# Delta-rule attention and a mixture of depths on one core: Gram matrices spilled from small buffers, corner blocks read back, inverses turned on VectorE, the first batches' experts last

## Chip, cores and metric

The kernel runs on one core of a Trainium2 chip. The metric is the device time of one execution in microseconds (us), the median of several runs.

## What is computed

The first block is a delta-rule recurrence over 768 steps for each of 4 batches and 8 heads, with a 48 x 48 state per head. The second gives the 128 best-scored tokens of each batch to a two-layer expert.

```python
k_n = k / (np.linalg.norm(k, axis=-1, keepdims=True) + 1e-06)
for t in range(S):                                   # state: (B, H, D, D)
    y[:, :, t] = einsum('bhd,bhde->bhe', q[:, :, t], state)
    v_old = einsum('bhde,bhd->bhe', state, kt)
    state = state + bt * einsum('bhd,bhe->bhde', kt, vt - v_old)
x = y.transpose(0, 2, 1, 3).reshape(B, S, H * D)     # (4, 768, 384)
scores = einsum('bsd,d->bs', x, w_gate)
for b in range(B):
    top = np.argpartition(-scores[b], 128)[:128]
    ye = np.maximum(x[b, top] @ w1, 0.0) @ w2        # 384 -> 1024 -> 384
    out[b, top] = x[b, top] + sigmoid(scores[b, top])[:, None] * ye
```

## The kernel before

**Units.** The sequence is cut into 12 chunks of 64 steps, and the batches into two groups (0 and 1, then 2 and 3). A unit `i` (0 to 23) is one chunk of one group: 16 pairs of batch and head, two to the 128 partitions. Within a chunk the delta rule is a triangular system. Its 64 x 64 matrix is inverted in two halves of 32: two 32 x 32 diagonal blocks and a corner block that couples them.

**Stages of a unit.** `prep` (L442) loads k and q, transposes them on TensorE (L433), forms the Gram matrix of k (`products`, L487; unit 0 to 3: `mm_g0`, L464 to L471), copies it to `g` (`out_g`, L494) and spills it to DRAM (`spill`, L499); it also forms q times k and masks it on VectorE (`out_p`, L503, into `p`). `eliminate` (L539) inverts the diagonal blocks of four units at once, so there are six eliminations, 0 to 5. It reads the blocks from DRAM with row and block index exchanged (`turn_in`, L553, into `a`; elimination 0 transposes on VectorE, L548), scales them (L559 to L584; a square root on ScalarE, L563), has ScalarE copy them into the PSUM bank pair `ap` (`lift`, L588) and runs 30 steps of a multiply and a subtract on VectorE (L600, L607). `final` (L613) multiplies by a table `mb` that GpSimd writes (L577), and `turn_out` (L616) transposes into `tt`. The inverse is needed in the other orientation too (`turn_back`): eliminations 0 and 5 transpose once more on VectorE (L621); eliminations 1 to 4 send it to DRAM (`ad`, L625) and back into `g` (`bring`, L630), and a third transfer copies the low blocks inside `tt` (`move`, L635). These three are called the round trip below. `join` (L670) makes the corner of the inverse for each unit with two products on TensorE, z (L692, L694) and j (L705, L707), and ScalarE copies (`ej`, L714). `recur` (L731) is the recurrence: R (L753, state times k), the add on VectorE (L760), W (L766, the inverse times v), ScalarE copies (L771), S (L777, the new state), copies (L784), and Q and P for the output (L793, L804, L810). Unit i needs unit i - 1's state.

**Ranking and experts.** Each unit's scores are taken (L827 on GpSimd, L831 on ScalarE) and compared with all earlier ones (`ranking`: rank products L898 and L900, compares L912 and L916 on GpSimd, L919 and L923 on VectorE, sums L940). Behind a group's last chunk its 128 tokens per batch are chosen (L982) and turned into indices by a product (L1000). `depths(b)` runs the expert of one batch: gather (L1021), turn (L1027), first product (L1037), second product (L1051), result (L1056), scatter (L1061).

**What sets the order.** All of this is entered as operations in a planner (`Plan`). Each has an engine, a duration, a priority and the ring buffers that it takes and gives back; the planner simulates the engines and writes each engine's instructions in one fixed order. Where TensorE would be idle it puts matmuls on a constant tile `warm` (fillers, L343). At run time each engine's queue is in order, and semaphores hold an instruction until its inputs are there.

**Buffers that matter here.** `g` has two places, each the Grams of a whole elimination, and a place is given back by the last join of that elimination (L670 on). `a` and `gd` have two places as well, `ad` two, `mb` one, `inv` three PSUM banks. `xe` (gathered tokens) has two places.

Of the kernel before, what the change touches and what calls it, by code (L numbers as in the profile page):

```python
# [15 lines left out]
P = 128  # L16
# [169 lines left out]
def kernel(  # L186
# [57 lines left out]
    ring("g", 2, [NB, C])  # L244
    ring("a", 2, [HC, HC])
    rings["gd"] = [dram.tile([P, NB, C], FP32, name=f"gd{m}") for m in range(2)]
    rings["ad"] = [dram.tile([2, HC, NB, HC], FP32, name=f"ad{m}") for m in range(2)]
    plan.ring("gd", 2)
    plan.ring("ad", 2)
    ring("mb", 1, [HC, HC])  # L250
# [8 lines left out]
    ring("xe", 2, [DM])  # L259
# [11 lines left out]
    plan.ring("boot", 2)  # L271

# [19 lines left out]
    bnat = const.tile([B * H, S], FP32, name="bnat")  # L292
# [60 lines left out]
    def constants():  # L353
# [13 lines left out]
        for t in rings["tt"]:  # L367
            nc.gpsimd.memset(t[:, :, :HC], 0.0)
# [73 lines left out]
    def prep(i):  # L442
# [32 lines left out]
        def out_g0(rt):  # L475
            def emit():
                nc.scalar.copy(
                    got("g", e)[:, n0:n0 + GP].rearrange("p (r b) t -> p r b t", b=2)[:, :, rt],
                    got(*kb)[rt][:, :GI * C].rearrange("p (r t) -> p r t", t=C))
            return emit  # L480
# [11 lines left out]
        def out_g(rt):  # L492
            def emit():
                nc.scalar.copy(got("g", e)[:, n0:n0 + GP]  # L494
                               .rearrange("p (r b) t -> p r b t", b=2)[:, :, rt], bank(kg[rt]))
# [27 lines left out]
        if first:  # L523
            n["g"] = pe(1.5, mm_g0, [n["ek"]], u, take=[kb] + [("g", e)] * (i == 0), hard=True,
                        ins=40 * GI)
            n["eg"] = [act(0.38, out_g0(rt), [n["g"]], u, give=[kb], hard=True)
                       for rt in range(2)]
        else:
            n["g"] = pe(0.55, products("kt", kg), [n["ek"], N[e * BC].get("g")], u, ins=16 * GI,
                        take=kg + [("g", e)] * (i % BC == 0))  # L530
            n["eg"] = [act(0.38, out_g(rt), [n["g"]], u, give=[kg[rt]]) for rt in range(2)]
            n["sg"] = sp(0.45, spill, n["eg"], u, take=[("gd", e)] * (i % BC == 0), moves=0.7,
                         dmas=1)
        v = 10 * i - 14
# [4 lines left out]
    def eliminate(e):  # L539
# [3 lines left out]
        near = first or e == NE - 1  # L543
        hard = dict(hard=first)

        def turn_in():
            if first:
                nc.vector.transpose(out=got("a", e),  # L548
                                    in_=got("g", e)[:, :, HC:].rearrange("p n t -> p t n"))
                return  # L550
            for par in range(2):
                for hf, rows in ((0, lo[par]), (1, hi[par])):
# [3 lines left out]
                        .rearrange("p n t -> n p t"))  # L556

# [70 lines left out]
        def bring():  # L628
            for par in range(2):
                nc.sync.dma_start(out=got("g", e)[lo[par], :, :HC], in_=got("ad", e)[par])  # L630

        def move():
            t = got("tt", e)
            for par in range(2):
                nc.sync.dma_start(out=t[lo[par], :, :HC], in_=t[lo[par], :, HC:])  # L635
# [4 lines left out]
        else:  # L640
            ti = sp(2.6, turn_in, [N[i]["sg"] for i in range(e * BC, (e + 1) * BC)], u,
                    take=[("a", e)], give=[("gd", e)], dmas=4, moves=0.83)
# [15 lines left out]
        last = dve(1.15, final, [last, s["mb"]], u, give=[] if near else [("mb", e)], **hard)  # L658
        N["final", e] = last
        s["to"] = dve(1.95, turn_out, [last], u, take=[("tt", e)], give=[("a", e)], **hard)  # L660
        if near:
            s["tb"] = dve(2.05, turn_back, [last], u, give=[("a", e)], hard=True)
        else:
            tb = sp(1.25, turn_back, [last], u, take=[("ad", e)], give=[("a", e)], dmas=2, moves=0.83)
            s["tb"] = sp(1.25, bring, [tb], u, give=[("ad", e)], dmas=2, moves=0.83)
# [475 lines left out]
```

## Time and profile before

| | us |
|---|---|
| median of 3 runs | 340.2 (338.43 to 340.38) |
| the profiled execution's own time | 336.96 |
| its span, first to last instruction | 335.2 |
| TensorE busy in the span | 308.9 |
| VectorE busy in the span | 207.6 |
| ScalarE busy in the span | 185.2 |
| GpSimd busy in the span | 104.4 |

In the profile PE is TensorE's matmuls, PEld its weight loads, DVE VectorE, ACT ScalarE, POOL GpSimd, and SP the SyncE queue that issues most DMAs. A row of groups names line, engine and operation, output and input tiles, shapes and count; then busy us and the mean of one in ns; then the engine's idle time just before, with what ended it. Busy matmuls overlap in their pipeline, so their busy time is more than their share of the queue.

### The profile page before, as it was taken

To read this page: it belongs to the slowest core of one execution; us is meant where nothing else is said; L and a number is where in the kernel's file an instruction comes from. 1 tells how busy PE (TensorE), PEld (TensorE's weight loads), DVE (VectorE), ACT (ScalarE), POOL (GpSimd) and SP (SyncE) were. 2 spreads that over 40 slices of the span, in tenths; PEclk is the share of its full clock that TensorE was granted. 3 is DMA by queue.
4 is the path that set the end of the run, shared out by engine and by line. 5 is a ranking of instruction groups with operands and counts; after the bars stand their busy time and mean duration, and the time that the engine had idled before them with its cause. 6 is when DMAs were issued, how large, how long until landed. Compare 5 with 4: busy or idle time off the path is not lost.

```text
span 335.2 us, 15324 instructions
## 1 busy us (share of the span) xinstructions
PE 308.9 (92%) x6678; PEld 231.5 (69%) x6678; DVE 207.6 (62%) x576; ACT 185.2 (55%) x508; POOL 104.4 (31%) x150
## 2 busy tenths in 40 slices
PE   7779999999879999989987999789999999999994
PEld 3665445788656778678864889656976888656782
DVE  6047998879769981798879796798840311252000
ACT  2445006776654666876785867863396688500110
POOL 8204001321360224404794232422021254802011
PEclk9969999999959999999977999989999999999998
DMA  7977991357793479767887268940050111201000
GB/s 132 140 130 184 179 344 42 56 137 176 126 170 62 94 178 164 134 132 195 158 151 135 55 176 151 164 89 10 23 117 7 43 34 49 49 2 47 2 23 23
DMA packets 130483, 35.89 MB, mean 107 GB/s; under 512 B 122832, under 2 KB 127056, under 8 KB 130416
## 3 DMA queue, kind: packets, MB, share of 16 engines
q1 hardware_dynamic: 127792, 32.95, 47.7%
q0 software_dynamic: 512, 1.57, 1.5%
q8 instruction: 52, 0.85, 1.0%
q10 hardware_dynamic: 2112, 0.39, 0.7%
q14 instruction: 15, 0.12, 0.1%
HBM read 22.05 MB, written 11.80 MB: 101 GB/s over the span
## 4 chain that ended last, share of the span: by engine, by line
PE 69%; ACT 10%; issue 7%; DVE 6%; POOL 4%; DMA 2%; SPq 0%; POOLq 0%; ACTq 0%; DVEq 0%
PE inv L343 16%; PE inv L433 7%; PE inv L487 7%; PE prec L766 6%; PE inv L1051 5%; PE psta L777 5%; PE prec L753 4%; PE inv L1037 4%; PE py L804 4%; PE py L793 3%; POOL mk L912 3%; ACT wbd L771 2%; DVE ap L607 2%; DVE tmp L600 2%; ACT tt L714 2%
## 5 line engine op out<-in xcount | busy, mean ns | idle before, releaser
L343 PE MATMUL inv<-warm 128*128 128x512 bf16 x282 | 71.8, 395 | 2.2 <-DVE warm L357 2.1
L607 DVE TENSOR_TENSOR ap<-ap,tmp 128x30 f32<-128x30 f32 (+9 forms) x180 | 60.7, 337 | 5.4
L600 DVE TENSOR_TENSOR tmp<-a,ap 128x30 f32<-128x30 f32 (+9 forms) x180 | 58.7, 326 | 5.4
L745 POOL TENSOR_TENSOR v<-v,nnT 128x384 f32<-128x384 f32 x24 | 20.0, 840 | 97.7 <-DMA v<-in_v_dram 61.5
L343 PEld LDWEIGHTS <-warm 128*128 128x128 bf16 x282 | 26.6, 101 | 30.0 <-issue 3.2
L827 POOL TENSOR_TENSOR prod<-x,wg 128x384 f32<-128x384 f32 x22 | 23.0, 1044 | 32.9 <-ACT x L810 28.4
L912 POOL TENSOR_SCALAR mk<-rep 128x64 bf16<-128x64 f32 (+11 forms) x22 | 27.5, 1249 | 15.9 <-ACT rep L904 8.2
L771 ACT COPY wbd<-prec 64x384 f32<-64x384 f32 x48 | 22.6, 472 | 14.1 <-PE prec L766 12.5
L714 ACT COPY tt<-inv 32x128 f32<-32x128 f32 x96 | 24.5, 255 | 9.0 <-PE inv L707 7.4
L760 DVE TENSOR_TENSOR v<-v,prec 128x384 f32<-128x384 f32 x22 | 12.2, 552 | 26.8 <-ACT x L810 15.0
L766 PE MATMUL prec<-v,tt 64*64 64x48 f32 x768 | 27.4, 220 | 0.7 <-DVE v L760 0.7
L766 PEld LDWEIGHTS prec<-v,tt 64*64 64x64 f32 x768 | 24.4, 134 | 5.2 <-DVE v L760 3.6
L1051 PE MATMUL inv<-w_sb,hT 128*128 128x384 f32 x64 | 24.2, 521 | 0.3 <-ACT tt L714 0.3
L784 ACT COPY s<-psta 64x384 f32<-64x384 f32 x44 | 20.8, 472 | 3.8 <-PE psta L777 3.2
L777 PE MATMUL psta<-wbd,k 128*48 128x96 f32 x352 | 19.1, 251 | 3.9 <-ACT wbd L771 3.5
L1037 PE MATMUL inv<-xeT,w_sb 128*128 128x128 f32 x192 | 22.5, 277 | 0.0
L1037 PEld LDWEIGHTS inv<-xeT,w_sb 128*128 128x128 f32 x192 | 21.7, 192 | 1.0 <-ACT xeT L1031 0.9
L503 DVE TENSOR_TENSOR p<-inv,up 128x256 f32<-128x256 f32 x48 | 19.1, 416 | 4.6 <-PE inv L487 3.2
L1056 DVE SCALAR_TENSOR_TENSOR oe<-inv,gate,xe 128x384 f32<-128x384 f32 x4 | 2.5, 618 | 31.0 <-PE inv L1051 31.0
L438 ACT COPY kt<-inv 128x512 f32<-128x512 f32 x24 | 14.0, 588 | 12.1 <-PE inv L433 12.0
L777 PEld LDWEIGHTS psta<-wbd,k 128*48 128x48 f32 x352 | 14.6, 122 | 8.7 <-ACT wbd L771 7.9
L804 PE MATMUL py<-wbd,p 128*64 128x96 f32 x384 | 20.5, 249 | 0.0
(142 smaller groups left out, 584.0 us busy)
## 6 DMA issues: line engine op xcount, KB each, us to landing
gd<-g SPq DMA_DIRECT2D x20, 256.0 KB, 3.1
v<-in_v_dram SPq DMA_DIRECT2D x48, 96.0 KB, 3.5
q<-in_q_dram SPq DMA_DIRECT2D x48, 96.0 KB, 3.4
k<-in_k_dram SPq DMA_DIRECT2D x44, 96.0 KB, 3.8
out_dram<-x SPq DMA_DIRECT2D x20, 192.0 KB, 2.8
a<-gd SPq DMA_DIRECT2D x20, 128.0 KB, 3.5
w_sb<-in_moe_w_dram SPq DMA_DIRECT2D x3, 512.0 KB, 4.5
w_sb<-in_moe_w_dram SPq DMA_DIRECT2D x4, 384.0 KB, 7.6
```

Source lines behind the costliest of these rows:

```text
L343: nc.tensor.matmul(rings[name][k], lhsT=warm[:, :P], rhs=warm, start=True, stop=True)
L433: nc.tensor.transpose(ps[:, r * P:(r + 1) * P], x[:, 2 * r:2 * r + 2].rearrange("p b d -> p (b d)"), ident)
L600: nc.vector.tensor_tensor(out=view(), op=ALU.mult, in0=got("a", e)[:, j + 1:, j:j + 1].to_broadcast([P, w, j]), in1=blocks[:, j:j + 1, :j] ...
L607: nc.vector.tensor_tensor(out=a[:, j + 1:, :j], in0=a[:, j + 1:, :j], in1=view(), op=ALU.subtract)
L714: nc.scalar.copy(to[lo[par], :, int(w == "jb"), HC:], view(w)[lo[par]])
L766: nc.tensor.matmul(pw[half[par], a], lhsT=tt[half[par], ch * GP + a], rhs=x[half[par], a], start=True, stop=True)
L771: nc.scalar.copy(wb[half[par], :, par], pw[half[par]])
L777: nc.tensor.matmul(psta[ds[a % 2], a // 2], lhsT=t[:, a, :D], rhs=wb[:, a].rearrange("p h d -> p (h d)"), start=(c == 0 and a < 2), stop=True,
L804: nc.tensor.matmul(pyv[half[bb], h4, rt], lhsT=t[:, a], rhs=wb[:, a], start=(c == 0 and h4 == 0 and rt == 0), stop=True, skip_group_check= ...
L912: nc.gpsimd.tensor_scalar(out=mk[:, :(j + 1) * C].rearrange("p (j c) -> p j c", c=C), in0=rep[:, :j + 1, :C], scalar1=rep[:, j, C:], scala ...
L1037: nc.tensor.matmul(got("inv", b, "h", f // 4)[:, f % 4 * CAP:(f % 4 + 1) * CAP], lhsT=w1_sb[:, t, f * P:(f + 1) * P], rhs=got("xeT", b)[:, ...
L1051: nc.tensor.matmul(got("inv", b, "o")[:CAP, :DM], lhsT=got("hT", b)[:, f], rhs=w2_sb[:, f], start=(f == 0), stop=(f == KF - 1))
```

## The change

Four things are changed.

1. The Grams of a unit go to one of four small places (`gs`, one unit each) and are spilled from there; a small place is free when its spill has landed. `gd` has a place for each elimination. Elimination 0's Grams lie in the second buffer of `tt`, whose low half GpSimd clears once their corners are used (`zeros`).
2. The corner blocks are read back from `gd` into `off` (`corner`), four DMAs an elimination, behind the `a` read.
3. The round trip is gone: in all eliminations VectorE transposes the inverse back into `mb` (two places now), and GpSimd copies the low blocks inside `tt` (`lows`, two copies a join; ScalarE did this in eliminations 0 and 5).
4. The experts of batches 0 and 1 get the priorities 400 to 406, behind everything, take the bank pair `ap` (ring `late`) and wait for the last elimination's `final`. `xe` has four places, so their tokens can be gathered early.

```diff
+    ring("gs", 4, [GP, C])
+    ring("off", 2, [BC * GI, HC])
     ring("a", 2, [HC, HC])
-    rings["gd"] = [dram.tile([P, NB, C], FP32, name=f"gd{m}") for m in range(2)]
...
+    rings["gd"] = [dram.tile([P, NB, C], FP32, name=f"gd{m}") for m in range(NE)]
...
+    rings["late"] = [ap[:, m] for m in range(2)]
+    plan.ring("late", 2)
+    first_g = rings["tt"][1]
...
         def spill():
-            nc.sync.dma_start(out=got("gd", e)[:, n0:n0 + GP], in_=got("g", e)[:, n0:n0 + GP])
+            nc.sync.dma_start(out=got("gd", e)[:, n0:n0 + GP], in_=got("gs", i))
...
+        def corner():
+            for par in range(2):
+                for rows, at, cols in ((hi[par], 0, slice(0, HC)), (lo[par], 1, slice(HC, C))):
+                    nc.sync.dma_start(out=got("off", e)[rows], in_=got("gd", e)[rows, at::2, cols])
...
         def turn_back():
-            if near:
-                nc.vector.transpose(out=got("mb", e).rearrange("p n t -> p t n"),
-                                    in_=got("a", e).rearrange("p i c -> p c i"))
-                return
-            for par in range(2):
-                nc.sync.dma_start(out=got("ad", e)[par].rearrange("i n k -> n i k"),
-                                  in_=got("a", e)[lo[par]])
...
+            nc.vector.transpose(out=got("mb", e).rearrange("p n t -> p t n"),
+                                in_=got("a", e).rearrange("p i c -> p c i"))
...
         def lows():
             t = got("tt", e)[:, n0:n0 + GP]
             for par in range(2):
-                nc.scalar.copy(t[lo[par], :, :HC], t[lo[par], :, HC:])
...
+                nc.gpsimd.tensor_copy(t[lo[par], :, :HC], t[lo[par], :, HC:])
...
-        u += du
...
+        u = u + du if g == NG - 1 else 400 + 4 * bb
+        tx = pe(0.4, turn_x, [ga] + [N["final", NE - 1]] * (g < NG - 1), u, take=[(bk, b, "xt"), ("xeT", b)], give=[("xe", b)],
```

SyncE, as elimination 2 ends, before: `a_107` is elimination 2's block, `a_108` elimination 3's, `gd_109` their spilled Grams.

```order
L499 DMA gd_109<-g_106 128x512
L422 DMA q_77<-in_q_dram 64x8x48 x2
L625 DMA ad_112<-a_107 32x32x32 x2
L815 DMA out_dram<-x_118 64x2x384 x2
L635 DMA tt_116<-tt_116 32x32x32 x2
L553 DMA a_108<-gd_109 32x32x32 x4
L630 DMA g_105<-ad_112 32x32x32 x2
L422 DMA k_69<-in_k_dram 64x8x48 x2
```

The same place after: `a_112` is elimination 3's block, `gd_115` its Grams, `off` the corners.

```order
L503 DMA gd_115<-gs_108 128x512
L426 DMA k_68<-in_k_dram 64x8x48 x2
L426 DMA q_76<-in_q_dram 64x8x48 x2
L812 DMA out_dram<-x_125 64x2x384 x2
L426 DMA q_77<-in_q_dram 64x8x48 x2
L556 DMA a_112<-gd_115 32x32x32 x4
L426 DMA k_69<-in_k_dram 64x8x48 x2
L426 DMA v_78<-in_v_dram 64x8x48 x2
L426 DMA q_75<-in_q_dram 64x8x48 x2
L564 DMA off_109<-gd_115 32x16x32 x4
```

The read of elimination 3's block stood behind two transfers that wait for elimination 2's end; now none of these is left, and the corners follow a few loads later.

VectorE, from the last steps of elimination 3 on, before (`a_108` is elimination 3's block, `a_107` elimination 4's, L760 the recurrence's add):

```order
L600 TENSOR_TENSOR tmp<-a_108,ap 128x30
L607 TENSOR_TENSOR ap<-ap,tmp 128x30
L613 TENSOR_TENSOR a_108<-ap,mb_113 128x1024
L616 STREAM_TRANSPOSE tt_117<-a_108 128x32x32
L946 TENSOR_TENSOR csum_154<-csum_154,inv_130 128x8
L559 TENSOR_SCALAR nrm<-a_107 128x32
```

The same place after (`a_112` is elimination 3's block, `a_111` elimination 4's; L575 to L579 are the small scalings, L592 is the scaling of the block):

```order
L579 TENSOR_TENSOR bh_168<-bh_168,bt 128x32
L615 TENSOR_TENSOR ap<-ap,tmp 128x30
L757 TENSOR_TENSOR v_83<-v_83,prec 128x384
L621 TENSOR_TENSOR a_112<-ap,mb_120 128x1024
L582 STREAM_TRANSPOSE nnT_166<-nrm 128x32
L624 STREAM_TRANSPOSE tt_124<-a_112 128x32x32
L628 STREAM_TRANSPOSE mb_120<-a_112 128x32x32
L592 TENSOR_TENSOR a_111<-a_111,bh_168 128x1024
```

Elimination 4's diagonal and small scalings have moved ahead of elimination 3's last step; the second transposition has come in.

TensorE behind the last W, after (W is L763; `ap` is written by the experts of batches 0 and 1, L1035 and L1049; before, fillers stood in these gaps):

```order
L763 MATMUL prec<-v_83,tt_124 64x48 x16
L895 MATMUL inv_138<-spr_128,pair 128x2x64
L897 MATMUL inv_138<-scr_158,ident 128x2
L790 MATMUL py<-s_173,qt_100 64x2x48 x8
L1049 MATMUL ap<-w_sb,hT_134 128x384
L801 MATMUL py<-wbd_172,p_104 64x96 x8
L895 MATMUL inv_137<-spr_128,pair 128x64
L897 MATMUL inv_137<-scr_158,ident 128x1
L1049 MATMUL ap<-w_sb,hT_134 128x384 x2
L1025 MATMUL ap<-ident,both 128x128 x3
```

Parts of the two late experts now stand between the rank products; the planner places 207 fillers in all, where it placed 282.

## Rows read from the trace of the kernel before

**Rows 1.** The page's first part: busy us (share of span) x instructions.

```profile
PE 308.9 (92%) x6678; PEld 231.5 (69%) x6678; DVE 207.6 (62%) x576; ACT 185.2 (55%) x508; POOL 104.4 (31%) x150
```

**Rows 2.** Windows: elimination 0's last transposition to elimination 5's.

```profile
core 0: us, PE busy (x) PEld busy (x) DVE busy (x) ACT busy (x) POOL busy (x), PEclk, DMA share, GB/s
54.30:245.60 191.30, 176.63 (x4574) 141.82 (x4572) 154.75 (x428) 130.33 (x358) 64.58 (x68) 0.96 0.60 122
```

**Rows 3.** Groups of TensorE in the window 54.3 to 245.6.

```profile
L343 PE MATMUL inv<-warm 128*128 128x512 bf16 x64 | 20.1, 420 | 0.1
...
L1037 PE MATMUL inv<-xeT,w_sb 128*128 128x128 f32 x96 | 11.2, 277 | 0.0
...
L1051 PE MATMUL inv<-w_sb,hT 128*128 128x384 f32 x16 | 7.1, 593 | 0.3 <-ACT tt L714 0.3
```

**Rows 4.** Groups of VectorE in the window 54.3 to 245.6.

```profile
L607 DVE TENSOR_TENSOR ap<-ap,tmp 128x30 f32<-128x30 f32 (+9 forms) x150 | 50.5, 337 | 4.4
L600 DVE TENSOR_TENSOR tmp<-a,ap 128x30 f32<-128x30 f32 (+9 forms) x150 | 48.9, 326 | 4.4
L503 DVE TENSOR_TENSOR p<-inv,up 128x256 f32<-128x256 f32 x39 | 15.7, 414 | 1.8 <-ACT mute L930 1.3 <-PE inv L487 0.4
...
L760 DVE TENSOR_TENSOR v<-v,prec 128x384 f32<-128x384 f32 x16 | 8.8, 552 | 8.4 <-ACT rep L904 3.9 <-PE prec L753 3.7 <-DMA v<-in_v_dram 0.5
...
L559 DVE TENSOR_SCALAR nrm<-a 128x32 f32<-128x32 f32 x4 | 0.7, 184 | 7.0 <-DMA a<-gd 7.0
L591 DVE MEMSET ap<- 128x32 f32 x5 | 0.4, 85 | 5.0 <-ACT ap L588 5.0
```

**Rows 5.** Timeline of VectorE: start, us, what, idle before.

```profile
52.29 2.00 DVE L621 STREAM_TRANSPOSE mb<-a 128x1024 f32<-128x1024 f32 x1
...
122.52 1.94 DVE L616 STREAM_TRANSPOSE tt<-a 128x1024 f32<-128x1024 f32 x1
...
133.90 0.19 DVE L559 TENSOR_SCALAR nrm<-a 128x32 f32<-128x32 f32 x1 [3.64 <-DMA a<-gd]
...
243.48 2.09 DVE L621 STREAM_TRANSPOSE mb<-a 128x1024 f32<-128x1024 f32 x1
```

**Rows 6.** DMA issues of the round trip: KB each, us to landing.

```profile
ad<-a SPq DMA_DIRECT2D x8, 128.0 KB, 3.4
...
g<-ad SPq DMA_DIRECT2D x8, 128.0 KB, 3.5
```

**Rows 7.** Timeline of TensorE: W of units 0, 20 and 23.

```profile
57.49 1.27 PE L766 MATMUL prec<-v,tt 64*64 64x48 f32 x32
...
267.13 1.08 PE L766 MATMUL prec<-v,tt 64*64 64x48 f32 x30
...
285.22 1.13 PE L766 MATMUL prec<-v,tt 64*64 64x48 f32 x32
```

**Rows 8.** TensorE from 285.2 on: the fillers' group, then timeline rows.

```profile
L343 PE MATMUL inv<-warm 128*128 128x512 bf16 x68 | 16.2, 379 | 0.0
...
306.67 0.49 PE L1027 MATMUL inv<-ident,xe 128*128 128x128 f32 x3
...
307.73 5.62 PE L1037 MATMUL inv<-xeT,w_sb 128*128 128x128 f32 x48
...
324.93 5.33 PE L1051 MATMUL inv<-w_sb,hT 128*128 128x384 f32 x16
```

**Rows 9.** Timeline: VectorE's scaling alone and beside GpSimd's table.

```profile
55.86 1.22 DVE L584 TENSOR_TENSOR a<-a,bh 128x1024 f32<-128x1024 f32 x1
...
92.42 1.26 POOL L577 TENSOR_SCALAR_AFFINE_SELECT mb<-bh 128x1024 f32<-128x1024 f32 x1 [3.67 <-DMA q<-in_q_dram]
...
92.73 2.02 DVE L584 TENSOR_TENSOR a<-a,bh 128x1024 f32<-128x1024 f32 x1
```

**Rows 10.** Groups of GpSimd by form: a fill of 1024 and a compare of 256.

```profile
L368 POOL MEMSET tt<- 128x1024 f32 x2 | 1.8, 950 | 0.0
...
L912 POOL TENSOR_SCALAR mk<-rep 128x256 bf16<-128x256 f32 x2 | 1.8, 920 | 0.0
```

More of the change, by code (lines that the diff above doesn't have):

```diff
@@ L258 @@
     ring("sel", 1, [NCH, CAP], BF16)
-    ring("xe", 2, [DM])
+    both = sbuf("both", [B, DM])
+    rings["xe"] = [both[:, m] for m in range(B)]
+    plan.ring("xe", B)
+    bnat = both[:B * H, :2].rearrange("p m d -> p (m d)")
+    assert S == 2 * DM
     ring("xeT", 1, [KD, CAP])
@@ L533, in prep @@
                          dmas=1)
+            plan.add("DMA", 0.0, lambda: None, [n["sg"]], u, give=[("gs", i)])
         v = 10 * i - 14
@@ L657, in eliminate, with zeros @@
         N["steps", e] = last
-        last = dve(1.15, final, [last, s["mb"]], u, give=[] if near else [("mb", e)], **hard)
+        last = dve(1.15, final, [last, s["mb"]], u, **hard)
         N["final", e] = last
[L660 to L665, printed above, removed]
-            s["mv"] = sp(1.25, move, [s["to"]], u, dmas=2, moves=0.83)
+        s["to"] = dve(1.95, turn_out, [last] + N.get("zeros", []), u, take=[("tt", e)],
+                      give=[("a", e)], **hard)
+        s["tb"] = dve(2.05, turn_back, [last], u, give=[("a", e)], hard=True)
         for m in range(BC):
             join(e, m)
+        def zeros():
+            for par in range(2):
+                nc.gpsimd.memset(first_g[hi[par], :, :HC], 0.0)
+        if first:
+            N["zeros"] = [pool(2.0, zeros, [N[m]["z"] for m in range(BC)], u + 20)]
     def join(e, m):
@@ L681, in view @@
             return got(*key[w])[:, :GI * HC].rearrange("p (n t) -> p n t", t=HC)
-        def back():
-            return got("mb", e) if near else got("g", e)[:, :, :HC]
         def z():
-            g, tt, tb, ps = got("g", e), got("tt", e), back(), view("z")
-            off = slice(0, HC) if first else slice(HC, C)
+            tt, tb, ps = got("tt", e), got("mb", e), view("z")
             for x in range(GI):
@@ L691, in z @@
                 for par in range(2):
[L692 removed]
+                    g, a, b = (first_g[:, :, :HC], na, na + 1) if first else (
+                        got("off", e), m * GI + x, m * GI + x)
+                    nc.tensor.matmul(ps[lo[par], x], lhsT=g[hi[par], a],
                                      rhs=tt[hi[par], na, HC:], start=True, stop=True)
[L694 removed]
+                    nc.tensor.matmul(ps[hi[par], x], lhsT=g[lo[par], b],
                                      rhs=tb[lo[par], na + 1], start=True, stop=True)
@@ L995, in depths @@
         g, bb = divmod(b, GB)
+        bk = "inv" if g == NG - 1 else "late"
         def mm_idx():
@@ L1089, in depths @@
             last = pe(0.66, mm_2(f), [hs[f // 4], last, N["w2", f // 2 * 2]], u, ins=4,
-                      take=[("inv", b, "o"), ("oe", b)] if f == 0 else [], give=[("hT", b)])
-        oo = dve(0.6, out_o, [last, g1], u, give=[("inv", b, "o"), ("xe", b)])
+                      take=[(bk, b, "o"), ("oe", b)] if f == 0 else [], give=[("hT", b)])
+        oo = dve(0.6, out_o, [last, g1], u, give=[(bk, b, "o"), ("xe", b)])
         pool(1.6, scatter, [oo], u, give=[("oe", b)])
```

69 lines of the change are left out of this document (27 added, 42 removed).

## The prediction, before the result was known

> **What bounds the kernel now.** The page's first part is read first: TensorE is busy for 92% of the span [rows 1]. That looks like a TensorE bound and is not one. The windows are read next, over 54.3 to 245.6, from the end of elimination 0's last transposition to that of elimination 5's: TensorE works 176.6 of 191.3 us, VectorE 154.8 [rows 2]. In the same stretch 64 of TensorE's matmuls are fillers on `warm` (20.1 us busy), and 11.2 and 7.1 us are the experts of batches 0 and 1 [rows 3]. Without these three it needs 138 us. VectorE has no filler: its 154.8 us are all needed, and the six eliminations follow one another on it, because each needs the bank pair `ap`. The groups of VectorE in that stretch show what its 36.5 idle us are [rows 4]: 4.4 + 4.4 gaps between the dependent steps, 7.0 waits for a block read back (`a<-gd`), 5.0 for ScalarE's lift into `ap`, 8.4 in front of the recurrence's add. In the timeline, elimination 2's last transposition starts at 122.52, and elimination 3 starts at 133.90 behind a wait of 3.64 for `a<-gd` [rows 5]. So until 245.6 the eliminations set the pace, with a fifth of that time lost around them.
>
> From there the end is serial. Unit 20's matmul on the inverse (L766, "W") starts at 267.13, 21.6 us after its inverse (243.48 + 2.09) and not 3.2 as in unit 0 (54.29 to 57.49) [rows 5, 7], because units 17 to 19 are late: TensorE had the experts of batches 0 and 1 in its queue between them. Unit 23's W is at 285.22 [rows 7]; from it to the span's end are 50.0 us: ranking, gather, and the experts of batches 2 and 3. In these 50 us TensorE runs 68 fillers, 16.2 us [rows 8]. This is room that the change wants to use.
>
> **The change, part by part.** *Spill from small places, a DRAM place for each elimination.* The Grams of the next elimination no longer wait until the joins of the one before last let go of a `g` buffer. On SP the read into `a` for elimination 3 stood behind the first and third transfer of elimination 2's round trip (L625, L635), which wait for that elimination's end; now it stands behind loads and an output write. On VectorE the diagonal and the scalings of eliminations 3 and 4 now stand among the last steps of the one before. I take the 7.0 us as gone, with 3.9 of the add's 8.4 (that wait lies in the same hole before 133.90) and 2.0 of the 5.0 for the lift, since in two eliminations of five the lift runs beside the transpositions. Idle left: 36.5 - 7.0 - 3.9 - 2.0 = 23.6. Bounds: 19 (the add's other 4.5 go too) and 36.5 (other waits take the place).
>
> *All inverses turned back by VectorE.* Four more transpositions of 2.0 us, the price of the two that are there (2.00, 2.09 [rows 5]): +8.2 on the bounding engine. In exchange the round trip through DRAM goes, two transfers in a row with 3.4 and 3.5 us from issue to landing each [rows 6], which lay on the path from an inverse to its first W, not on VectorE. Into the window also move five products `p` of 0.414 and two adds of 0.552 from behind elimination 5 [rows 4]: +3.2. VectorE then needs 154.8 + 8.2 + 3.2 + 23.6 = 189.8 instead of 191.3, and elimination 5 ends at 54.3 + 189.8 = 244.1. TensorE can follow: its 138 us, and 15 for two more units (138 / 18 = 7.7 each), are less than that.
>
> *Corner reads.* Four reads an elimination for the six transfers of the round trip. They are issued behind the `a` read, an elimination ahead of use. I price them at nothing; their cover is some 30 us of steps. If it went, the cost would be one landing, 3.5 us, an elimination.
>
> *Copies of the low blocks on GpSimd.* Forty-eight, two a join; 16 ScalarE copies and 8 transfers go. No row shows this copy: 256 elements cost between 0.24 us (the fill rate, 950 ns for 1024) and 0.92 (the compare on 256) [rows 10]; I take 0.5, 4 us for the eight of an elimination. W of the first unit needs the first two alone, 1 us behind the transposition, beside the second transposition's 2 us: hidden. What else can they cost? VectorE's scaling took 2.02 us instead of 1.22 where GpSimd's table had started just before it [rows 9]. Read from these rows alone, every VectorE instruction beside a copy could stretch by 1.65, over 8 x 0.5 = 4 us an elimination: up to 2.6 each, 13 over five. Nearest is the row of the scaling, at 0.8 once an elimination, which the 154.8 holds in part; I take nothing.
>
> The Trainium skill (SBUF — State Buffer, "Who interferes with whom") narrows this: a Vector instruction with two SBUF inputs contends with a GpSimd one that reads SBUF, one with a single SBUF input outside its two-port modes does not. The steps read one operand from PSUM, so by that rule only the scaling can stretch: 0.8 an elimination, 4 us in all, and the sum would be 4 us longer at most. The two rows agree with it; no row has a step beside a copy.
>
> *From elimination 5 to the end.* Unit 20's W came 3.2 us behind unit 0's inverse; in the new order three groups of batch 0's first product (0.70 each, an eighth of 5.62 [rows 8]) stand among the joins; one lies beside VectorE's transpositions, 0.5 of the others in waits for ScalarE, 0.9 is added: W at 244.1 + 4.1 = 248.2, before 267.13. Unit 23's W was 18.1 us later. New between them are 15 rows of that product (an expert's 24 in the order are 5.62 us, so 3.5), one join's z and two j (1.2 together, estimated from the two joins between 54.29 and 57.49); three rank products (0.5 each, an estimate from the turn's 0.49) and eight fillers of 0.24 go (3.4), 0.2 comes in small sums: 18.1 + 1.5 = 19.6, W at 267.8, before 285.22.
>
> Behind it the new order has batch 1's first product and both second products: 5.62 + 2 x 5.33 + 0.5 for a turn [rows 8] = 16.8. Out go 62 of 67 fillers at 16.2 / 68 = 0.24 (14.8) and one sum (0.7): +1.3, and 0.7 for waits that no longer fit: 52.0. End at 267.8 + 52.0 = 319.8, before 335.2: **15.4 us less**.
>
> The profiled execution took 336.96, 1.8 beside its span; the median of the runs shown is 340.2. The difference is carried over: 340.2 - 15.4 = **324.8 us**.
>
> **Rivals.** *VectorE keeps its waits.* The hole before 133.90 is filled by the second transposition and by others: idle stays 36.5, 12.9 more, 337.7. For it: the add waits for a recurrence that is itself late; against it: what held `a` on SP, the round trip, is gone.
>
> *The late experts are not hidden.* Ranking goes through TensorE, VectorE, ScalarE and GpSimd in turn, and the queues are in order; batch 0's result (L1054) even stands between two count sums on VectorE. If the 16.8 us fit only into the gather's gap (from the index product to the turn at 306.67, some 5 us), 11.8 is added: 336.6. Against it: 62 fillers stood in just these gaps.
>
> *The read-back comes late.* This is the one on the other side. The place is SP: the reads of `a` stand behind loads that wait for `k` and `q` buffers, and behind output writes that wait for recurrences. If each of eliminations 2 to 5 loses what elimination 3 lost, from 124.46 (the end of the transposition at 122.52) to 133.90 [rows 5], 9.4 us, that is 37.6: 324.8 + 37.6 = 362. It decides from about 5 us an elimination (19 in all). For it: 7.0 us of such waits in the profile [rows 4]; against it: the wait before 133.90 was 3.64 net, and its cause, the round trip ahead of the read on SP, is taken out.
>
> *Better still.* VectorE idle 19 (4.6 less), and 3.2 more because the runs may sit where the profiled execution does: 317.
>
> **Chances.** The sum as told 0.66, its own range 320 to 333 (idle 19 to 32). Waits stay 0.12. Experts exposed 0.10. Read-back late 0.07. Better 0.05, with a low end of 314 if the tail gives 3 as well. About 1% (3.4 us) is what a measurement of this kernel can tell from no change, so faster is below 336.8. The first and the last are faster; so is half of the second and third (0.11); 0.10 of these is within 1%; 0.07 and 0.01 are slower. The range takes in the second and third, and leaves out the fourth: 314 to 338.
>
> **What would show it.** Right: the last VectorE transposition of elimination 5 ends between 240 and 250; no wait for `a<-gd` over 1 us; unit 20's W within 5 us of that end; unit 23's W near 268; under 10 fillers behind it, and 51 to 53 us to the end. In the new order both early exponentials stand behind ScalarE's last square root, so its square-root table is loaded once less. Wrong: VectorE idle above 30 us in its window; GpSimd's copies over 1 us each, with ScalarE's copies into `tt` waiting for them; index product more than 18 us behind the last W; a granted clock of 1.2 GHz for long in the last stretch.

## The result and the profile after

The kernel after takes 330.8 us, the median of four runs (330.3 to 332.9), beside 340.3 for the kernel before on the same chip: a ratio of 0.974, 95% interval 0.968 to 0.980. Some executions lie over 1.5% above the fastest of their kernel, most of them at a lower granted clock; the ratios leave them out, the medians and ranges do not. Forecast were 324.8 us, 15.4 less; it is 9.5 less. The profiled executions differ by less: 336.96 before (3.3 below its median) and 330.42 after (0.4 below). Their spans are 335.2 and 328.6, so a sum that was made against the trace, for which 319.8 was forecast, is short by 8.8 us. Carrying the difference over to the median hid 3 us of that.

The first part of the page after, then the windows: elimination 0's last transposition to elimination 5's, from there to W of unit 23, and the rest. To be held against [rows 1, 2].

```profile
PE 294.1 (90%) x6583; PEld 229.5 (70%) x6603; DVE 210.3 (64%) x580; ACT 177.1 (54%) x490; POOL 126.5 (39%) x199
```

```profile
core 0: us, PE busy (x) PEld busy (x) DVE busy (x) ACT busy (x) POOL busy (x), PEclk, DMA share, GB/s
55.44:246.77 191.33, 171.99 (x4791) 142.46 (x4802) 160.34 (x442) 134.57 (x377) 89.66 (x117) 0.95 0.54 114
246.77:274.02 27.25, 25.48 (x682) 23.13 (x682) 3.69 (x12) 18.21 (x56) 11.60 (x18) 0.94 0.12 29
274.02:329.00 54.98, 47.43 (x405) 35.11 (x406) 10.78 (x34) 10.04 (x24) 10.15 (x10) 0.99 0.10 30
```

The first window is as long as before (191.3 [rows 2]); VectorE is busy 5.6 us more in it and idle 31.0 instead of 36.5. In the last two windows TensorE is busy 72.9 of 82 us, and of the other 9 some 5 lie behind its last matmul: from elimination 5 on it has hardly a gap. The groups of VectorE in the first window, to be held against [rows 4]:

```profile
L615 DVE TENSOR_TENSOR ap<-ap,tmp 128x30 f32<-128x30 f32 (+9 forms) x150 | 50.4, 336 | 4.0
L608 DVE TENSOR_TENSOR tmp<-a,ap 128x30 f32<-128x30 f32 (+9 forms) x150 | 48.7, 325 | 3.9
...
L628 DVE STREAM_TRANSPOSE mb<-a 128x1024 f32<-128x1024 f32 x6 | 12.2, 2028 | 0.0
L757 DVE TENSOR_TENSOR v<-v,prec 128x384 f32<-128x384 f32 x19 | 10.5, 553 | 13.0 <-PE prec L750 10.5 <-POOL prod L824 1.3 <-DMA a<-gd 0.8
...
L592 DVE TENSOR_TENSOR a<-a,bh 128x1024 f32<-128x1024 f32 x5 | 6.3, 1258 | 0.1
...
L575 DVE TENSOR_SCALAR nrm<-nrm 128x32 f32<-128x32 f32 x5 | 1.3, 255 | 1.0 <-ACT nrm L571 1.0
...
L567 DVE TENSOR_SCALAR nrm<-a 128x32 f32<-128x32 f32 x4 | 0.8, 202 | 0.7 <-DMA a<-gd 0.7
L599 DVE MEMSET ap<- 128x32 f32 x5 | 0.4, 85 | 6.8 <-ACT ap L596 6.8
```

The wait for a block read back fell from 7.0 to 0.7 (0.8 more is put down to it in front of an add). The wait in front of the recurrence's add rose from 8.4 to 13.0, and most of it, 10.5 (before 3.7), is now for R, the product on TensorE (L750); the wait for ScalarE's lift rose from 5.0 to 6.8. These sums hide where the waits lie. From transposition to transposition VectorE was idle for 5.9, 5.5, 12.6, 5.1 and 7.6 us in eliminations 1 to 5; after, it is 5.7, 7.5, 4.5, 6.5 and 6.8. The windows of elimination 3, before and after, and the row before that waited longest in it:

```profile
124.46:168.64 44.18, 41.62 (x1166) 34.93 (x1163) 31.59 (x89) 33.56 (x96) 19.75 (x21) 1.00 0.79 158
```

```profile
133.94:167.81 33.87, 29.92 (x871) 24.75 (x874) 29.39 (x82) 23.66 (x69) 15.27 (x18) 1.00 0.64 137
```

```profile
128.91 0.55 DVE L760 TENSOR_TENSOR v<-v,prec 128x384 f32<-128x384 f32 x1 [3.87 <-ACT rep L904]
```

This hole has closed. The timelines of VectorE and of TensorE give the ends of the stages:

```profile
242.82 2.13 DVE L628 STREAM_TRANSPOSE mb<-a 128x1024 f32<-128x1024 f32 x1
244.86 1.91 DVE L624 STREAM_TRANSPOSE tt<-a 128x1024 f32<-128x1024 f32 x1
```

```profile
251.69 1.17 PE L763 MATMUL prec<-v,tt 64*64 64x48 f32 x32
...
274.02 1.14 PE L763 MATMUL prec<-v,tt 64*64 64x48 f32 x32
...
282.21 0.91 PE L1049 MATMUL ap<-w_sb,hT 128*128 128x384 f32 x2 [0.57 <-ACT xeT L1029]
283.05 0.76 PE L937 MATMUL inv<-warm,mk 64*64 64x1 bf16 x38
283.74 2.20 PE L1049 MATMUL ap<-w_sb,hT 128*128 128x384 f32 x6
285.88 0.51 PE L937 MATMUL inv<-warm,mk 64*64 64x1 bf16 x22
...
291.66 1.60 PE L1035 MATMUL ap<-xeT,w_sb 128*128 128x128 f32 x12 [0.69 <-ACT hT L1042]
293.20 0.67 PE L998 MATMUL inv<-tok,sel 64*128 64x2 bf16 x24
...
296.07 4.14 PE L1049 MATMUL ap<-w_sb,hT 128*128 128x384 f32 x12 [0.69 <-ACT hT L1042]
300.05 0.49 PE L1025 MATMUL inv<-ident,both 128*128 128x128 f32 x3
```

| us | before | forecast | after | after, second trace |
|---|---|---|---|---|
| elimination 0 ends | 54.3 | 54.3 | 55.4 | 55.2 |
| from there to elimination 5's end | 191.3 | 189.8 | 191.3 | 193.8 |
| from there to W of unit 20 | 21.6 | 4.1 | 4.9 | 4.3 |
| W of unit 20 to W of unit 23 | 18.1 | 19.6 | 22.3 | 20.9 |
| last W to the end of the span | 50.0 | 52.0 | 54.6 | 54.6 |

The rows of TensorE show where the last stage grew. Rank sums (L937) and the index product (L998) are a few tenths of a us each, but each stands in the queue behind pieces of the late experts (L1035, L1049), and some of these wait for ScalarE themselves. The choice on VectorE ended at 291.13, the index product ran at 293.20. It came 19.2 us behind the last W; before, 16.1. And before, GpSimd had three compares to begin behind the last W, the one of 512 first; now it has two:

```profile
286.66 1.56 POOL L912 TENSOR_SCALAR mk<-rep 128x512 bf16<-128x512 f32 x1
```

```profile
276.55 1.72 POOL L909 TENSOR_SCALAR mk<-rep 128x576 bf16<-128x576 f32 x1 [8.36 <-ACT rep L901]
```

The turn of batch 2's tokens at 300.05 then stood behind twelve matmuls of batch 1's second product: 6.9 us behind the index product, before 5.4.

### The profile page after: what moved, and what is told of

Same layout as the page of the kernel before. It is cut to its first block, busy times and chain, and to the rows that moved or that the text cites. A ratio compares the mean times of both kernels' runs of the same rounds, so it can differ in the third digit from the quotient of the medians.

```text
span 328.6 us, 15204 instructions
## 1 busy us (share of the span) xinstructions
PE 294.1 (90%) x6583; PEld 229.5 (70%) x6603; DVE 210.3 (64%) x580; ACT 177.1 (54%) x490; POOL 126.5 (39%) x199
## 4 chain that ended last, share of the span: by engine, by line
PE 66%; issue 10%; ACT 8%; DVE 6%; POOL 5%; DMA 2%; SPq 1%; POOLq 0%; ACTq 0%; DVEq 0%
PE inv L348 13%; PE prec L763 6%; PE inv L437 6%; PE inv L491 5%; PE psta L774 5%; PE py L801 4%; PE ap L1035 4%; PE py L790 4%; PE prec L750 4%; PE ap L1049 3%; POOL mk L909 3%; ACT wbd L768 2%; PE inv L701 2%; PE inv L1035 2%; PE inv L1049 2%
## 5 line engine op out<-in xcount | busy, mean ns | idle before, releaser
L348 PE MATMUL inv<-warm 128*128 128x512 bf16 x187 | 51.3, 401 | 5.3 <-DVE warm L362 2.1
L824 POOL TENSOR_TENSOR prod<-x,wg 128x384 f32<-128x384 f32 x22 | 23.9, 1088 | 37.4 <-ACT x L807 37.2
L742 POOL TENSOR_TENSOR v<-v,nnT 128x384 f32<-128x384 f32 x24 | 19.7, 828 | 47.0 <-DMA v<-in_v_dram 46.9
L348 PEld LDWEIGHTS <-warm 128*128 128x128 bf16 x207 | 19.8, 102 | 23.0 <-issue 3.3
L716 POOL COPY tt<-tt 32x256 f32<-32x256 f32 x48 | 19.5, 406 | 25.4 <-DVE tt L624 21.1
L763 PEld LDWEIGHTS prec<-v,tt 64*64 64x64 f32 x768 | 25.2, 138 | 4.8 <-issue 2.4
L763 PE MATMUL prec<-v,tt 64*64 64x48 f32 x768 | 28.1, 223 | 0.3
L774 PE MATMUL psta<-wbd,k 128*48 128x96 f32 x352 | 21.5, 268 | 3.8 <-ACT wbd L768 2.9
L774 PEld LDWEIGHTS psta<-wbd,k 128*48 128x48 f32 x352 | 16.5, 133 | 9.4 <-ACT wbd L768 6.2
L801 PE MATMUL py<-wbd,p 128*64 128x96 f32 x384 | 21.8, 260 | 0.0
L585 POOL TENSOR_SCALAR_AFFINE_SELECT mb<-bh 128x1024 f32<-128x1024 f32 x6 | 11.6, 1941 | 24.9 <-DVE bh L579 24.9
L442 ACT COPY kt<-inv 128x512 f32<-128x512 f32 x24 | 14.1, 591 | 13.1 <-PE inv L437 12.9
L790 PE MATMUL py<-s,qt 128*64 128x96 f32 x352 | 20.1, 260 | 0.0
L801 PEld LDWEIGHTS py<-wbd,p 128*64 128x64 f32 x384 | 18.7, 147 | 1.2 <-ACT spr L890 0.5
## 6 DMA issues: line engine op xcount, KB each, us to landing
gd<-gs SPq DMA_DIRECT2D x20, 256.0 KB, 2.9
```

What stands on the lines that cost most here:

```text
L348: nc.tensor.matmul(rings[name][k], lhsT=warm[:, :P], rhs=warm, start=True, stop=True)
L763: nc.tensor.matmul(pw[half[par], a], lhsT=tt[half[par], ch * GP + a], rhs=x[half[par], a], start=True, stop=True)
L774: nc.tensor.matmul(psta[ds[a % 2], a // 2], lhsT=t[:, a, :D], rhs=wb[:, a].rearrange("p h d -> p (h d)"), start=(c == 0 and a < 2), stop=True,
L790: nc.tensor.matmul(pyv[half[bb], h4, :, par], lhsT=qt[:, bb * 2 + h4, half[par]], rhs=s_old[:, bb * 2 + h4, par], start=(h4 == 0 and par = ...
L801: nc.tensor.matmul(pyv[half[bb], h4, rt], lhsT=t[:, a], rhs=wb[:, a], start=(c == 0 and h4 == 0 and rt == 0), stop=True, skip_group_check= ...
L824: nc.gpsimd.tensor_tensor(out=got("prod", i), in0=got("x", i // 2)[:, i % 2], in1=wg, op=ALU.mult)
```

## The experiments

All ran with runs of the kernel before on the same chip; ratios are to these.

**The late experts alone**, in the kernel before. Theory A was the prediction's: the hole of 21.6 us in front of unit 20's W comes from the experts in TensorE's queue.

```diff
+    rings["late"] = [ap[:, m] for m in range(2)]
...
+        u = u + du if g == NG - 1 else 400 + 4 * bb
```

> The kernel before with the fourth part alone: the experts of batches 0 and 1 last of all, in the bank pair ap, with four places for the gathered tokens. Theory A (the gain is the experts' move; the rest of the change only trades one VectorE time for another): 326 to 333 us, W of unit 20 within 10 us of elimination 5's end, which stays near 245.6. Theory B (units 16 to 19 were late because of the round trip and of the shared g buffers, not because of the experts): 337 to 342 us, W of unit 20 still 15 us or more behind elimination 5.

334.2 us (332.1 to 336.8), ratio 0.983 [0.975, 0.991]: between the two. W of unit 20 came 7.1 us behind elimination 5, as A has it, but elimination 5 ended at 251.4, not near 245.6. Elimination 0 ended 1.9 later, and the window grew from 191.3 to 195.2. The profiled run was the slowest of the four (336.8).

**All but the late experts**: the kernel after with `depths` as before.

```diff
-        u = u + du if g == NG - 1 else 400 + 4 * bb
+        u += du
```

> The kernel after with the experts of batches 0 and 1 back where they were (priorities, banks, no wait for the last elimination); parts one to three stay. Theory A: 337 to 343 us, W of unit 20 again 15 us or more behind elimination 5, whose end is within 3 us of 246.8. Theory B: 328 to 334 us, W of unit 20 within 8 us of elimination 5.

335.1 us (334.5 to 340.7), ratio 0.988 [0.979, 0.996]. W of unit 20 is again 19.7 us behind elimination 5, which ends at 244.9, as A said; yet the time is 2 us below A's bound. The first three parts are worth some 5 us by themselves, which A did not have.

**The inverses turned back by VectorE, low blocks on ScalarE**, in the kernel before.

```diff
-    ring("mb", 1, [HC, HC])
+    ring("mb", 2, [HC, HC])
...
-        near = first or e == NE - 1
+        near = True
```

> The kernel before with all six inverses turned back by VectorE (mb gets a second place) and the low blocks copied by ScalarE in all joins; g and gd stay shared, the experts stay early. Theory A: the four transpositions (8.2 us) come on top and the waits for a<-gd (7.0) shrink only in part, so elimination 5 ends 1 to 8 us later and the time is 341 to 348. Theory B (the round trip was what made units late): 330 to 336.

The four runs took 338.9, 340.8, 346.9 and 347.3 us; the first is the profiled one. The median, 343.9, is A's time, but the two lower runs are no longer than the kernel before beside them (340.1): a cost is not shown. Nor did it go A's way: elimination 5 ended at 244.5, not later than before, with all four transpositions more. VectorE's idle time shrank by 5.3 us, to 31.3: of its groups between 54.5 and 244.5 the waits for R and for the read are the ones that fell, to 3.2 and 3.9, and ScalarE's rose.

```profile
L760 DVE TENSOR_TENSOR v<-v,prec 128x384 f32<-128x384 f32 x16 | 8.7, 547 | 3.2 <-PE prec L753 3.0 <-issue 0.2
...
L567 DVE TENSOR_SCALAR nrm<-nrm 128x32 f32<-128x32 f32 x5 | 0.9, 174 | 5.4 <-ACT nrm L563 5.4
...
L559 DVE TENSOR_SCALAR nrm<-a 128x32 f32<-128x32 f32 x4 | 0.7, 185 | 3.9 <-DMA a<-gd 3.9
```

What this gained was lost behind elimination 5: W of unit 20 came at 271.1, 26.5 us after it.

**The low blocks on ScalarE in the kernel after.**

```diff
-                nc.gpsimd.tensor_copy(t[lo[par], :, :HC], t[lo[par], :, HC:])
+                nc.scalar.copy(t[lo[par], :, :HC], t[lo[par], :, HC:])
...
```

> The kernel after with the 48 copies of low blocks on ScalarE instead of GpSimd. If GpSimd's copies are hidden and hurt nothing (my pricing): ScalarE gets 48 copies of some 0.4 us more, 329 to 333, no change that can be measured. If the copies on GpSimd stretch VectorE or make joins wait: 325 to 328. If ScalarE is now the engine that VectorE waits for (lift, square root): 333 to 338.

336.6 us (334.1 to 340.2), ratio 0.9885 [0.979, 0.998]: the third case. Elimination 5 ends at 256.0, 9.2 us later (6.9 later than in the second trace of the kernel after). The groups of VectorE from 55.3 to 256:

```profile
L575 DVE TENSOR_SCALAR nrm<-nrm 128x32 f32<-128x32 f32 x5 | 0.9, 172 | 8.4 <-ACT nrm L571 8.4
...
L567 DVE TENSOR_SCALAR nrm<-a 128x32 f32<-128x32 f32 x4 | 0.7, 172 | 3.2 <-DMA a<-gd 3.2
...
L599 DVE MEMSET ap<- 128x32 f32 x5 | 0.4, 85 | 6.7 <-ACT ap L596 5.7 <-ACT junk L828 1.0
```

The square root waits in ScalarE's queue: 8.4 us, in the kernel after 1.0. So the engine of the 48 copies matters. The prediction had their time on GpSimd, but no term for what they take off ScalarE. On GpSimd a copy takes 406 ns (0.5 were taken):

```profile
L716 POOL COPY tt<-tt 32x256 f32<-32x256 f32 x48 | 19.5, 406 | 25.4 <-DVE tt L624 21.1
```

**The kernel after again.** This gives the last column of the table above.

> The kernel after, unchanged, as the mark for the three runs beside it: 329 to 333 us; elimination 5 ends near 246.8, W of unit 20 some 5 us behind it, the index product 19 us behind the last W, the end 54 to 55 behind it. If these stages differ by more than 1.5 us from the first trace, what I read from single traces is chance.

331.2 us (330.6 to 332.3), ratio 0.969 [0.965, 0.972]. The stages agree within 1.5 us but for the window of the eliminations, which is 2.5 longer; from the last W on, nothing differs by 0.1. By the expectation's own measure, a difference of 2.5 us or less in that window between single traces is chance.

**The experts of batches 0 and 1 left out.**

```diff
+        if g < NG - 1:
+            return
         ga = pool(1.1, gather, [xi] + [N["put", (g * NCH + j) // 2] for j in range(NCH)], u,
```

> The kernel after with the experts of batches 0 and 1 left out (their gather, two products, result and scatter; these tokens keep their attention output). Theory A (what the forecast missed behind elimination 5 is the price of the late experts, whose matmuls stand in front of the ranking in TensorE's queue): W of units 20 to 23 take 17 to 19 us instead of 22.3, the index product comes 16 to 17 us behind the last W instead of 19.2, the tail is 49 to 51 us instead of 54.6, the time 321 to 326. Theory B (it is the half clock of TensorE and the experts themselves are hidden): tail and spacing stay within 1.5 us, 328 to 333.

320.4 us (318.1 to 321.2), ratio 0.936 [0.931, 0.940]: 10.7 us less than the kernel after beside it. From its timeline of TensorE:

```profile
250.98 1.88 PE L763 MATMUL prec<-v,tt 64*64 64x48 f32 x32
...
270.88 1.13 PE L763 MATMUL prec<-v,tt 64*64 64x48 f32 x32
...
284.99 0.67 PE L998 MATMUL inv<-tok,sel 64*128 64x2 bf16 x24
```

The index product is 14.1 us behind the last W (19.2 with the experts), the span's end (318.7) 47.8 (54.6), both below A's bounds, as is the time; the three units take 19.9, somewhat above. Theory A, then, and in the tail more than it asked: placed last, the two experts still cost 10.7 us, 6.8 of them in the tail.

**More fillers where the clock falls.** In the page's windows of the kernel after the granted clock is 0.92 during elimination 5. By the clock's record it is at its lower level, 1.2 GHz, from 211.7 to 218.5 (TensorE was busy for 4.2 of the 5 us from 205 to 210); the add of unit 16, at 220.34, then waits 2.88 us for R.

```diff
+        if e in (3, 4, 5):
+            key = ("inv", "keep", e)
+            pe(0.22 * 12, lambda: filler(*plan.live[key], 12), [last], u + 20, take=[key],
+               give=[key], ins=2 * 12)
```

> The kernel after with twelve more fillers behind the last multiply of eliminations 3, 4 and 5, in the hole in which TensorE waits for the transpositions and behind which its granted clock fell to half (170.7, 211.7 and 256.0 us). If half clock is what makes the recurrence late there (the adds' waits of 2.4 and 2.9 us, the 9.8 us from W of unit 20 to that of unit 21): fewer us at half clock between 160 and 262 (20.5 before), those waits at 1.5 or less, 325 to 329 us. If half clock costs nothing on the path, or the fillers don't move it: 330 to 335.

329.7 us (327.8 to 331.1), ratio 0.964 [0.959, 0.968], 1.4 below the kernel after: no change that can be told. The windows of elimination 5, of the kernel after and of this one (the second fence), columns as above:

```profile
205.10:246.80 41.70, 37.78 (x998) 32.21 (x998) 34.86 (x100) 29.35 (x82) 18.58 (x26) 0.92 0.39 74
```

```profile
206.90:248.80 41.90, 37.21 (x1046) 31.32 (x1047) 34.77 (x104) 30.07 (x85) 20.17 (x29) 1.00 0.43 84
```

The clock stays at 1.00 (2.4 GHz), and the adds wait 1.1 us in it instead of 3.3. The window is as long as it was: VectorE waits 2.3 for the read and 1.0 for an exponential instead. A wait on VectorE that went was taken up by others here; in all fourteen traces VectorE is idle for 5.9 to 8.5 us in elimination 5. The lower clock was real, but it was not what made this stretch long. Behind elimination 5 it does cost time. From W of unit 20 to that of unit 21, the kernel after in its first trace and in its second:

```profile
251.69:261.49 9.80, 8.45 (x259) 7.72 (x250) 1.05 (x4) 6.61 (x22) 2.77 (x4) 0.83 0.02 3
```

```profile
253.35:261.69 8.34, 6.91 (x260) 6.30 (x251) 1.05 (x4) 6.79 (x24) 2.63 (x5) 1.00 0.02 4
```

The same instructions take 1.5 us longer in the trace in which the clock fell (from 256.0 to 259.5); with the added fillers it is 7.9 us at 1.00, in the next run, without them, 9.4 at 0.82.

**Ranking first.**

```diff
-            hd = dict(hard=last)
+            hd = dict(hard=last or soon)
...
-                             give=[("sel", g)], ins=2 * NCH)
+                             give=[("sel", g)], ins=2 * NCH, hard=g == NG - 1)
```

> The kernel after with the last group's ranking products and its index products marked as urgent in the planner, so that matmuls of the late experts are put in front of them only where they fit: three pieces of batch 1's first product move behind the index product. Theory A: index product 17 to 18.5 us behind the last W (19.2), of which half comes back in the gather's hole; 328.5 to 330.5 us. Theory B (the waits lie elsewhere): index product stays at 19, 330 to 333.

328.9 us (325.2 to 329.7), ratio 0.960 [0.954, 0.966], 2.2 below the kernel after; the intervals of the two ratios just touch. The index product came 17.1 us behind the last W, 2.1 sooner, and the tail is 53.8 instead of 54.6: theory A, with over half of it given back behind the index product, where the same matmuls are now in the way.

**Both edits.**

> The kernel after with both edits: the fillers behind the last multiply of eliminations 3 to 5, and the last group's ranking and index products marked urgent. If the two small gains are real and add up: 326.5 to 328.5 us, a ratio to before of 0.955 to 0.962. If either was chance, or both fill the same hole: 329 to 331.

327.2 us (325.8 to 330.2), ratio 0.964 [0.958, 0.969]. The time is in the expected range, the ratio is not, and it is not below that of either edit alone. That they add up is not shown. In its trace the index product comes 16.9 us behind the last W, but the turn only 8.4 us behind that, and the tail is 55.0.

**The experts left out of the kernel before.** The edit is that of the run on the kernel after.

> The kernel before with the experts of batches 0 and 1 left out (as in the run on the kernel after; their tokens keep the attention output). In after they still cost 10.7 us. Theory A (early, between units 16 and 20, nearly all of their TensorE time lay on the path): they cost 15 to 20 us here, 321 to 326 us, and W of unit 20 comes within 6 us of elimination 5's end. Theory B (units 16 to 19 were late because of the round trip): 330 us or more.

327.8 us (327.1 to 328.1), ratio 0.9635 [0.958, 0.969]. It lies between the theories: early, the experts cost 12.8 us, not 15 to 20; and without them W of unit 20, at 260.9, is still 12.8 us behind elimination 5 (248.1). What holds it is in the timelines of TensorE (W of unit 19) and ScalarE:

```profile
248.58 1.14 PE L766 MATMUL prec<-v,tt 64*64 64x48 f32 x32
```

```profile
249.25 1.68 ACT L720 COPY tt<-tt 32x256 f32<-32x256 f32 x4
250.95 1.08 ACT L714 COPY tt<-inv 32x128 f32<-32x128 f32 x4
...
252.35 0.83 ACT L720 COPY tt<-tt 32x256 f32<-32x256 f32 x2
...
253.36 0.47 ACT L771 COPY wbd<-prec 64x384 f32<-64x384 f32 x1
253.73 1.08 ACT L714 COPY tt<-inv 32x128 f32<-32x128 f32 x4
254.72 0.47 ACT L771 COPY wbd<-prec 64x384 f32<-64x384 f32 x1
```

W of unit 19 was done at 249.72. Its two copies (`wbd`), which the next state needs, ran at 253.36 and 254.72, behind copies of low blocks (L720) and of joins. They were done 5.5 us behind the product, at unit 21 it is 1.0: ScalarE's queue has 4.5 of the 6.5 us by which the step from unit 19 to unit 20 (12.3) is longer than the next (5.8). This is read from the trace; no run takes these copies alone out of that queue. It also needs a unit that is still outstanding: with late experts (first run) and the same copies on ScalarE, W of unit 19 came before elimination 5's end, and unit 20's 7.1 us behind it.

**The turning alone, with GpSimd's copies, and the same with late experts.** This is the edit on the kernel before, then on the one with late experts; Grams, their DRAM places and corners stay as before. `mb` has two places.

```diff
-        near = first or e == NE - 1
+        near = True
...
-                nc.scalar.copy(t[lo[par], :, :HC], t[lo[par], :, HC:])
+                nc.gpsimd.tensor_copy(t[lo[par], :, :HC], t[lo[par], :, HC:])
```

> The kernel before with all six inverses turned back by VectorE and the low blocks copied by GpSimd in all joins; g, gd and the experts as before. It is the third part of the change alone. Theory A (the 5 us that parts one to three gave with the early experts come from the turning, but only with GpSimd's copies, since with ScalarE's copies it cost 4): 334 to 337 us. Theory B (they need the small places and the corner reads too): 338 to 343.

> The same with the experts of batches 0 and 1 last of all: the whole change but for the small places, the six gd places and the corner reads. Theory A: 329.5 to 333 us, as the kernel after. Theory B: 334 to 338.

336.4 us (334.6 to 338.0), ratio 0.988 [0.979, 0.997], and 326.0 (323.2 to 333.7), ratio 0.954 [0.941, 0.966]. Theory A in the first, though the 4 us that its expectation sets out from are not shown (see the run with ScalarE's copies); in the second the time is below A's range. The small places and the corner reads are worth nothing that can be seen, with early experts (0.988 and 0.988) or late ones (0.954 without them, 0.974 and 0.969 with them; whether they cost something stays open, the interval of the last overlaps a little). The wait for the read falls without them too, from 7.0 to 1.5:

```profile
L559 DVE TENSOR_SCALAR nrm<-a 128x32 f32<-128x32 f32 x4 | 0.7, 186 | 1.5 <-DMA a<-gd 1.5
```

So most of it was the round trip. The second run has the lowest time of all that compute the whole, below before and after, though its four runs lie far apart. The windows of the eliminations, first with early experts, then with late ones:

```profile
54.10:240.40 186.30, 170.79 (x4516) 142.06 (x4527) 160.29 (x433) 127.59 (x351) 81.32 (x109) 0.93 0.50 107
```

```profile
54.25:246.50 192.25, 172.31 (x4826) 145.28 (x4837) 162.99 (x444) 136.13 (x384) 89.63 (x119) 0.94 0.51 109
...
270.46:323.20 52.74, 46.25 (x402) 34.32 (x404) 10.72 (x34) 8.84 (x22) 10.14 (x10) 0.99 0.10 31
```

With the turning alone the eliminations end 5.2 us earlier than before (240.4), and W of unit 20 does not follow until 267.1. With the late experts it follows within 4.6 us (251.1), but the eliminations take 6 us longer. Where the times come from is another matter. In the first trace W of unit 23 is only 0.4 us sooner than before, and 2.0 of the 2.4 us by which its span is shorter lie behind it, where GpSimd has two compares left instead of three. The second trace is 5.5 us shorter than that of the kernel after, 4.9 of it behind W of unit 20 (19.3 to unit 23, then 52.6), where nothing is spilled or read back any more.

| ratio to before | experts early | last | left out |
|---|---|---|---|
| first three parts as before | 1 | 0.983 | 0.964 |
| turning with GpSimd's copies | 0.988 | 0.954 | |
| all three parts | 0.988 | 0.974, 0.969 | 0.936 |

## Why the prediction was right in part

*Right:* the direction and, within the range, the size; that the hole in front of unit 20's W closes (4.9 us, 4.1 forecast); that the wait for `a<-gd` goes (0.7), though it goes with the round trip and not with the small places, under which it stood; that the window of the eliminations is no longer with four more transpositions in it, though by errors that cancelled (see below). Three fillers are left behind the last W, and ScalarE loads its square-root table once less (before at 209.1). Two of the signs of being wrong came: VectorE idle above 30 us (31.0), and an index product more than 18 us behind the last W (19.2), the one that was named for late experts in the way. GpSimd's copies were hidden and stretched little: the steps took 325 and 336 ns (326 and 337 before), and the ten of 300 that overlapped a copy were no longer than the others; the scaling took 1258 instead of 1526, the one that overlapped a copy 1403. The Trainium skill (SBUF — State Buffer, "Who interferes with whom") says that a Vector instruction with a single input in SBUF, outside its two-port modes, does not contend with GpSimd; these ten steps agree.

*Wrong, the idle time of VectorE.* The sum had 36.5 - 7.0 - 3.9 - 2.0 = 23.6; it is 31.0, and 33.5 in the second trace. What was struck out did go: the hole of elimination 3 fell from 12.6 to 4.5 (6.5 in the second trace); the 3.9 of the add's wait, for `rep`, stands in no row any more; the lift's waits fell by 1.9 in two eliminations. But other waits came, which the sum put at nothing: for R, 2.8, 0.6, 1.6, 2.4 and 3.1 us in eliminations 1 to 5 (before 1.4, 0, 0.7, 1.6 and 0), and 3.7 more for the lift in the other three eliminations. I had taken idle time as a sum of separate waits of which each can be struck out, with nothing in its place. The busy time came out lower, 160.3 instead of 166.2: the 11.4 were added from mean durations, but neighbours on VectorE overlap (the last transposition starts at 244.86, the one before it ends at 244.95), and where the durations rose by 9.2, the busy time rose by 5.6. The two errors nearly cancelled in the window (191.3, forecast 189.8); that it agrees is luck.

The other waits come in part with the experts' move. Late experts lengthen the eliminations: by 3.9 on the kernel before (195.2 against 191.3), by 6.0 on the turned one (192.3 against 186.3), by 2.0 and 4.5 on the one with all three parts (191.3 and 193.8 against 189.3). Without these experts they are longer as well, by 3.0 (194.3 against 191.3) and 3.2 (192.5 against 189.3), so it is the lack of early experts that does it: units 16 to 19 are no longer late then, their adds and products fall into elimination 5, and on VectorE's queue an add that waits for R holds the next step. Part of what the move gains is given back there; how much can't be told from single traces that lie 2.5 apart. With the turning alone, experts early, the idle time is 26.0, not far from the sum's.

*Wrong, the price of the late experts.* "16.8 of matmuls in the place of 62 fillers, +1.3, and 0.7 for waits" was the term mis-sized: +2.0 forecast, +4.6 measured in the tail. Against the run without them it is +6.8 (54.6, 47.8), since the rest of the tail had become 2.2 shorter. Without late experts the index product is 14.1 us behind the last W in the four traces with two compares left, 16.1 in the two with three. Nor is it one price: in the eight traces with late experts, in their different orders, the tail is 52.6 to 57.4. Between units 20 and 23, +1.5 was forecast and +4.2 and +2.8 came; without the experts it is still +1.8, and the two traces differ by the clock between units 20 and 21. A filler has no inputs to wait for and the planner puts it where nothing is ready. A piece of an expert waits for ScalarE's copies, in the same in-order queue as the rank products, and what the plan takes for a gap is not one when the engines run at other times than planned. The rival of late experts not hidden had this mechanism at 11.8 us over the forecast; 2.6 of that came true in the tail. Left out, the two experts give back 10.7 us.

*Wrong in part, the cause of the 21.6 us hole.* It was put down to the experts alone. Moved last, they let it shrink to 7.1, so they are most of it; but they were 12.8 us of the time, and with them gone W of unit 20 still came 12.8 behind elimination 5, mostly for the joins' copies in ScalarE's queue. That GpSimd's copies take work off ScalarE stood in the diff, and had no term; put back on ScalarE they cost the kernel after some 5.7 us. By the times the turning with GpSimd's copies is worth some 1% with early experts (interval 0.3 to 2.1) and 3% with late ones, where the sum booked 8.2 us of VectorE to it and the waits that go to the small places. By which way it gains is not shown: with early experts W of unit 20 is at 267.1 in both traces, and what is gained lies behind it.

*Small:* the first elimination ended 1.1 us later. The seven other traces that begin with the same three parts have its end between 54.3 and 55.6, so this may be chance.

## What to carry to other kernels

Before work is moved into gaps that fillers hold, ask what each moved instruction waits for, and what stands behind it in its in-order queue; a gap is worth less to work with inputs than to a filler. Waits of an engine that several chains share are not to be struck out one by one: those that were priced went here, and others came elsewhere (12.9 us struck out, 5.5 gained), so ask for each stage which chain is late next. A shared stage also has to be compared with what it would cost in the same order: the rest of the tail had become shorter, and this hid a third of what the late experts cost there. And when an engine loses work (here ScalarE's copies), look at what its queue holds up at the narrowest place of the kernel, even if it is idle for almost half of the time.

## What was not expected of the hardware

TensorE's granted clock fell to 1.2 GHz for 3.4 to 10.2 us at a time in the kernel after, at 170.7 behind a wait of 3.5 us for ScalarE's copy of q. With the added fillers two of the three falls between 160 and 262 are gone; the one at 256.0 is missing in the second trace without them too, so only the one in elimination 5 can be put down to them, and elimination 5 stayed as long as before. What a fall costs depends on the stage: nothing that shows there, 1.5 us between units 20 and 21. On ScalarE two copies of low blocks take 0.83 us, 0.41 each, the same as on GpSimd (406 ns): it was the queue that differed, not the copy.
